# Global queries of two batches instead of one at the end, value copies on the chip for eight pairs, and a new order

## The chip, the cores and the metric

The kernel runs on one core of a Trainium2 chip. The metric is the device time of one execution in microseconds (us). In the profile the engines are PE (TensorE, matrix products), DVE (VectorE), ACT (ScalarE), POOL (GpSimd) and SP (SyncE, which here does nothing but issue DMA transfers).

## The reference

Two layers in float32. The first is attention over 8 batches and 8 heads of width 64, with 32 global and 512 local tokens per head: a global query sees everything, a local query sees the 32 global keys and the local keys at most 32 positions away. The second layer multiplies two projections of the result and sends the product through two more weights.

```python
s_g   = scale * q_g @ concat(k_g, k_l).T          # 32 x 544 a head
out_g = softmax(s_g) @ concat(v_g, v_l)
s_ll  = where(|i - j| <= 32, scale * q_l @ k_l.T, -1e9)
out_l = softmax(concat(scale * q_l @ k_g.T, s_ll)) @ concat(v_g, v_l)
x     = concat(out_g, out_l) as (8 * 544 tokens, 512)
out   = (((x @ w1) * (x @ w2)) @ w3) @ w_out      # w1, w2 512x1024, w3 1024x1024, w_out 1024x512
```

## The kernel before, in words

**Weights.** `w3 @ w_out` is folded into one 1024x512 matrix on the chip: `fold` (L690 to L693), 64 steps of two matmuls each, into 8 tiles that are then split in a high and a low float32r part (`w34h`, `w34l`, L695). The weights come packed (`fetch`, 512 KB a tile for w3 and wo); each tile is unpacked (`unit`) by a shift on DVE (L603), an activation on ACT (L605) and a shift-and-or on DVE (L607), where w1 and w2 are split as well (by further `unit` steps).

**Pairs.** A pair m is two heads of one batch (m = 0 to 31, batch m // 4). For each pair SP loads q, k and v. `kc` (L320 to L324) spreads K into shifted windows in two copies; `vc` (L309 to L314) spreads the global V in two copies. The values also need V shifted by 32 rows either way: for pairs below `VC` this is made on the chip by four copies `vs` (L297 to L304, two large ones of 32x1536 and two small ones of 32x384 elements), for the others by four more DMA transfers (L292 to L295). `s` is the scores (L348, 64 short matmuls), `mm` and `ex` the minimum on DVE and the exponential on ACT, eight of each. For pairs below `TP` the weights are turned by PE (`tp`) and copied out (`pt`); for the others by DVE and a round trip through DRAM (`tn`, `po`, `pi`). `v` is the values (L400, 64 short matmuls), `nm` the division; for pairs below `XT` `xt` turns the result on PE (four transposes), for the others DVE and DRAM do (`vn`, `vw`, `vi`). `xh` and `xl` split it in two float32r parts, the input of the second layer.

**Global queries.** They are worked two pairs at a time (u = m // 2): `sg` scores (L471, 48 matmuls), `gq`, `gr`, `ge` minimum and exponential, `gt`, `go`, `gi` the turn through DRAM (`gi` is the read-back, L381), `vg` values (L500 and L505), `gn`, `gd` division and write-out. They need K and V of their pairs on the chip. They run for m from `LATE` to 31 together with the pairs; those of the first `LATE` pairs are done at the end of the program as m = 32 and up, for which K and V are loaded and spread again (`keys`). When all are written, `gin` reads the global tokens back, and `gxh` and `gxl` split them.

**Second layer.** 17 blocks k of at most 256 tokens, 4 groups each. `first` (L546 to L548) is a step of 12 gate matmuls, in which w1 and w2 meet x; `ga`, `gb_`, `gh`, `gl` copy one half, multiply and split (ACT and DVE); `second` (L576 to L578) sends the product through the folded matrix; `out` and `store` write it out. Block 15 is the global tokens, block 16 the last local ones.

**What sets the order.** Nothing is scheduled at run time. `ORDER_OF` gives each step of each kind a position in one common order of the program, 0 to 2516; a letter A, D or P before it chooses ACT, DVE or POOL. Each engine carries out its own steps in rising position and waits wherever a step's input, or the buffer that it writes to, is not ready. SP issues all transfers in this order too, so one that waits holds up those behind it. Buffers are rings of fixed length: K 2, V 3, q 2, raw weights 3. `warm` is 20 matmul records on a cleared tile (`clear`, L250) that have no use in the result. The lines that set how much runs where:

```python
LAG, TP, XT, LATE, VC = 1, 4, 4, 4, 4                      # L27
        nc.sync.dma_start(V[32:64], src)                   # L289
        if m < VC:
            return
        nc.sync.dma_start(V[0:32, 1:4], src[:, 0:3])       # L292, and three more
        for part in range(4 * (m < VC)):                   # L745
            add(("vs", m, part), "POOL ACT DVE", [("load", "v", m)], shift_v, m, part)
    for m in range(NM + LATE):                             # L972, NM = 32 pairs
        if m < NM:
            pair(m)
        if m >= LATE:
            global_pair(m)
```

## Time and profile before

| | |
|---|---|
| median of 3 runs | 761.49 us (755.45 to 762.23) |
| the profiled execution | 756.57 us, of which its span is 754.8 us |
| PE busy | 736.7 us (98% of the span) |
| weight loads of PE (overlapping) | 644.5 us (85%) |
| DVE busy | 424.5 us (56%) |
| ACT busy | 272.9 us (36%) |
| POOL busy | 116.8 us (15%) |
| moved by DMA | 133.95 MB, 177 GB/s on the mean |
| instructions | 24101 |

The span runs from the first to the last instruction that the profile shows; the execution's own time is 1.8 us longer. A share of busy time is a mean over stages with different limits, so it says which engine to look at and not where the time goes. A busy PE is one that has matmuls in its pipe; since their ends are modelled, it may still run below its peak. A line of a group such as "x40 | 16.0, 404 | 1.1 <-DVE mn L355 1.0" reads: 40 instructions, 16.0 us busy, 404 ns each on the mean, 1.1 us of idle time of the engine ahead of them, 1.0 of which ended when DVE wrote `mn` on L355.

### The profile page before, as it was taken

The page shows a single profiled execution, that of the slowest core. Times are in us where ns is not written, and L with a number is a line of the kernel's source. Part 1 is how long each engine was busy: PE and PEld are TensorE (multiplying, and loading weights), DVE is VectorE, ACT ScalarE, POOL GpSimd, SP SyncE. Part 2 cuts the span into 40 slices and gives each one's busy share as a digit, 9 for nine tenths or more (in the row PEclk, how much of TensorE's full clock was granted, in tenths as well). Part 3 has the DMA queues.
Part 4 walks back from the last instruction along what each step waited for, and adds up shares of the span by engine and source line. Part 5 has one row for each costly group of instructions (what it writes and reads, how often), then busy time and mean ns, then how long its engine had stood idle before and what let it go on. Part 6 is the DMA issues. An engine that isn't in the chain of part 4 may idle for free.

```text
span 754.8 us, 24101 instructions
## 1 busy us (share of the span) xinstructions
PE 736.7 (98%) x10036; PEld 644.5 (85%) x10036; DVE 424.5 (56%) x1264; ACT 272.9 (36%) x839; POOL 116.8 (15%) x174
## 2 busy tenths in 40 slices
PE   4989999999999999999999999999999999999998
PEld 3345598999998998989989999999988999999997
DVE  4787887756555457555675645656554455424232
ACT  4677876533244232213334333442323321210000
POOL 2034533110102110200201120102100111110000
PEclk9999999999999999999999999999999999999999
DMA  8997787786678483957575677667593848210000
GB/s 282 303 291 273 179 244 218 213 245 198 173 198 238 127 219 93 256 144 193 144 218 171 169 209 229 198 182 196 144 244 104 242 138 218 76 45 29 1 29 29
DMA packets 98037, 133.95 MB, mean 177 GB/s; under 512 B 15848, under 2 KB 58472, under 8 KB 97928
## 3 DMA queue, kind: packets, MB, share of 16 engines
q1 hardware_dynamic: 97928, 132.41, 61.6%
q8 instruction: 79, 1.29, 0.8%
q14 instruction: 30, 0.25, 0.1%
HBM read 94.62 MB, written 37.75 MB: 175 GB/s over the span
## 4 chain that ended last, share of the span: by engine, by line
PE 94%; DMA 3%; DVE 1%; issue 1%; ACT 0%; SPq 0%; DVEq 0%; ACTq 0%
PE bp L546 9%; PE ap L546 9%; PE acc L576 9%; PE bp L547 8%; PE acc L578 8%; PE bp L548 8%; PE acc L577 8%; PE ap L548 8%; PE ap L547 8%; PE w L693 5%; PE s L348 4%; PE v L400 4%; PE sg L471 2%; DMA raw_wo<-in_wo_t_dram 2%; PE gx L500 2%; DMA raw_w<-in_w_t_dram 2%
## 5 line engine op out<-in xcount | busy, mean ns | idle before, releaser
L546 PE MATMUL bp<-x,w12h 128*128 128x256 f32 x512 | 144.5, 282 | 0.0
L546 PE MATMUL ap<-x,w12h 128*128 128x256 f32 x512 | 144.3, 282 | 0.0
L547 PE MATMUL bp<-x,w12h 128*128 128x256 f32 x512 | 142.4, 278 | 0.2 <-issue 0.2
L548 PE MATMUL bp<-x,w12l 128*128 128x256 f32 x512 | 142.2, 278 | 0.0
L547 PE MATMUL ap<-x,w12h 128*128 128x256 f32 x512 | 142.2, 278 | 0.0
L548 PE MATMUL ap<-x,w12l 128*128 128x256 f32 x512 | 142.1, 277 | 0.0
L360 ACT ACTIVATE P<-P,mn 128x128 f32<-128x128 f32 x256 | 100.7, 396 | 44.4 <-issue 24.3
L546 PEld LDWEIGHTS bp<-x,w12h 128*128 128x128 f32 x512 | 96.2, 188 | 4.7 <-issue 2.4
L546 PEld LDWEIGHTS ap<-x,w12h 128*128 128x128 f32 x512 | 96.1, 188 | 4.1 <-issue 1.6
L547 PEld LDWEIGHTS bp<-x,w12h 128*128 128x128 f32 x512 | 96.3, 188 | 2.0 <-issue 0.4
L547 PEld LDWEIGHTS ap<-x,w12h 128*128 128x128 f32 x512 | 96.2, 188 | 1.6
L548 PEld LDWEIGHTS ap<-x,w12l 128*128 128x128 f32 x512 | 96.5, 189 | 0.0
L548 PEld LDWEIGHTS bp<-x,w12l 128*128 128x128 f32 x512 | 96.5, 189 | 0.0
L355 DVE CUSTOM_DVE_ANT_0 P<-s,cs 128x128 f32<-128x128 f32 x256 | 62.7, 281 | 35.1 <-PE s L348 34.5
L693 PE MATMUL w<-wo,w3f 128*128 128x512 f32 x128 | 59.5, 603 | 5.3 <-issue 3.0
L314 POOL COPY V<-vg 32x1024 f32<-32x1024 f32 x35 | 37.0, 1065 | 135.4 <-PE gx L500 68.3
L693 PEld LDWEIGHTS w<-wo,w3f 128*128 128x128 f32 x128 | 22.7, 190 | 32.3 <-issue 24.5
L360 ACT ACTIVATION_READ_ACCUMULATOR P<-P,mn 128x1 f32 x256 | 48.9, 191 | 0.0
L348 PE MATMUL s<-K,q 64*32 64x128 f32 x2048 | 37.8, 278 | 8.9 <-DVE w3f L607 8.8
L348 PEld LDWEIGHTS s<-K,q 64*32 64x32 f32 x2048 | 29.1, 107 | 18.3 <-issue 13.6
L324 POOL COPY K<-K 128x480 f32<-128x480 f32 x26 | 16.1, 632 | 136.4 <-DMA K<-in_kp_t_dram 129.4
L416 DVE TENSOR_TENSOR vo<-v,si 128x512 f32<-128x512 f32 x32 | 22.0, 687 | 24.8 <-PE v L400 21.4
(786 smaller groups left out, 1355.7 us busy)
## 6 DMA issues: line engine op xcount, KB each, us to landing
Pd<-P SPq DMA_DIRECT2D x112, 128.0 KB, 2.6
Pt<-Pd SPq DMA_DIRECT2D x28, 512.0 KB, 4.9
raw_w<-in_w_t_dram SPq DMA_DIRECT2D x24, 512.0 KB, 5.8
V<-in_v_t_dram SPq DMA_DIRECT2D x64, 192.0 KB, 4.3
K<-in_kp_t_dram SPq DMA_DIRECT2D x36, 272.0 KB, 3.9
V<-in_v_t_dram SPq DMA_DIRECT2D x36, 256.0 KB, 4.0
out_dram<-o SPq DMA_DIRECT2D x34, 256.0 KB, 3.3
q<-in_q_t_dram SPq DMA_DIRECT2D x32, 256.0 KB, 4.3
```

Of the source, the lines that this page charges most:

```text
L314: (nc.scalar.copy if eng is nc.scalar else eng.tensor_copy)(to, src)
L348: nc.tensor.matmul(block(st[:, h], x, 128 * g), q[64 * h : 64 * h + 64, c : c + 32], window(m, h, 4 * g + x), start=True, stop=True, skip_ ...
L355: nc.vector.tensor_tensor_reduce(T["P", m][:, :, h, g], chunks(T["s", m][:, h, 128 * g : 128 * g + 128]), chunks(masks[g]), -0.125, 3.0e38 ...
L360: nc.scalar.activation(P, P, AF.Exp, bias=T["mn", m][:, g, h : h + 1], scale=-1.0, accum_out=T["sm", m][:, g, h : h + 1])
L400: nc.tensor.matmul(vt[32 * x : 32 * x + 32, g, h], t[:, x, h, g], Vs[m % NV][:, x, h, g], start=True, stop=True, skip_group_check=True)
L546: nc.tensor.matmul(d, wh[:, k, c, :], x[:, 0, 0:w], start=(k == m % 2 == 0), stop=False, skip_group_check=True)
L547: nc.tensor.matmul(d, wh[:, k, c, :], x[:, 1, 0:w], start=False, stop=False, skip_group_check=True)
L548: nc.tensor.matmul(d, wl[:, k, c, :], x[:, 0, 0:w], start=False, stop=(k == 3), skip_group_check=True)
L576: nc.tensor.matmul(a, gh[:, m % 2, sl], wh, start=(m == 0), stop=False)
L577: nc.tensor.matmul(a, gh[:, m % 2, sl], wl, start=False, stop=False)
L578: nc.tensor.matmul(a, gl[:, m % 2, sl], wh, start=False, stop=(m == 7))
L693: nc.tensor.matmul(T["w34", t], T["w3f", t, j // 4][:, j % 4], T["wo"][:, j], start=(j == 0), stop=(j == 7))
```

## The change

Two constants change, and with them how many steps of some kinds there are, so the whole of `ORDER_OF` is written anew. No function changes.

- `LATE` 4 to 8: the global queries of batches 0 and 1 (u = 16 to 19), instead of those of batch 0 alone (u = 16, 17), stand at the end. The K, V and global V of eight pairs instead of four are loaded and spread a second time, and qg of batch 1 is loaded late.
- `VC` 4 to 8: pairs 4 to 7 get their shifted V by four copies each instead of four transfers. Reloaded pairs (m of 32 and up) still take the transfers.
- The new order has 2558 steps (2517 before): SP 377 (368), POOL 174 (152), ACT 554 (550), DVE 870 (864), PE 583 (583). Engine letters move too: `vs` is now on ACT 15 times, DVE 4, POOL 13 (8, 2, 6); `kc` 24, 21, 35 (29, 17, 26); `vc` 30, 20, 30 (21, 16, 35); `xl` is 22 on DVE and 42 on POOL (37 and 27).

```diff
-LAG, TP, XT, LATE, VC = 1, 4, 4, 4, 4
+LAG, TP, XT, LATE, VC = 1, 4, 4, 8, 8
...
-    clear="13 2 44",
-    edges="20",
-    warm="22",
...
-    vs="A149 P174 P173 A140 A120 D111 A157 D131 A200 A191 P253 P236 A351 P292 P248 A288",
...
-    sg="440 628 741 885 994 1131 1266 1386 1525 1653 1788 1906 2033 2170 2245 2313",
...
-    gi="609 740 853 1021 1094 1256 1405 1542 1641 1740 1898 2021 2159 2251 2305 2359",
-    vg="659 776 886 1048 1136 1279 1449 1573 1652 1758 1917 2057 2171 2276 2316 2360",
...
-    gin="2371 2376 2401 2404",
...
+    clear="12 4 24",
+    edges="27",
+    warm="18",
...
+    vs="A136 D145 A61 P213 A105 P221 D124 D87 P260 A208 A258 P198 A327 P372 P344 D362 P474 A504 P416 A396 P493 A489  "
+    "P423 P532 P664 A540 A639 A546 A691 A628 A680 P602",
...
+    v="217 265 335 392 514 594 685 741 800 866 905 973 1071 1096 1164 1242 1312 1387 1459 1500 1580 1670 1704 1774  "
...
+    sg="743 870 1009 1125 1238 1395 1517 1638 1787 1897 2025 2153 2218 2279 2331 2385",
...
+    gi="825 966 1122 1227 1357 1491 1659 1721 1903 2021 2125 2234 2290 2337 2376 2411",
+    vg="865 983 1126 1240 1389 1501 1663 1770 1942 2050 2152 2242 2297 2339 2393 2424",
...
+    gin="2439 2445 2452 2459",
```

The new lists of `vs` stand pair after pair, four to a pair, so those of pair 4 are P474, A504, P416 and A396, and its values stand at 514. Four stretches of the orders, position and step (a step is named by its kind, then pair or tile, then part):

```
SP before   0 w3.0.0  1 k.0  4 vg.0  5 w3.3.0  6 constants  7 q.0  8 k.1  9 w3.1.0  10 wo.0  18 w3.2.0  29 wo.4  30 wo.1
SP after    0 w3.0.0  2 wo.0  3 vg.0  6 k.0  7 k.1  13 constants  16 q.0  17 w3.3.0  20 w3.1.0  23 w3.2.0  26 wo.1  28 wo.2
PE before   19 s.0  22 warm  48 fold.3.0  49 fold.0.0  57 fold.1.0  ...  185 s.2  192 v.0  ...  440 sg.2  442 first.0.0.0
PE after    18 warm  31 fold.0.0  32 s.0  54 fold.1.0  56 fold.1.1  ...  200 s.2  209 fold.4.1  217 v.0  ...  454 first.0.0.0
ACT after   473 ga.0  477 kc.7.0  482 unit.w12s.4.2.4  484 ex  485 ex  489 vs.5.1  490 ex  502 unit.w12s.5.0.2  504 vs.4.1
PE end, before   2313 sg.17  2316 vg.16  ...  2360 vg.17  ...  2461 first.16.0.0
PE end, after    2385 sg.19  2393 vg.18  ...  2424 vg.19  ...  2465 first.15.0.0
```

Between sg.19 and vg.19 PE has seven steps of `first`, four of `second` and vg.18; between sg.17 and vg.17 before it had seven and five, and vg.16. The sizes of the transfers at the start: a w3 or wo tile 512 KB, k 272, q 256, constants 112, vg 64.

## Rows read from the trace of the kernel before

**Rows 1.** Busy time by stretch (start:end, length; PE, weight loads, DVE, ACT, POOL; clock, DMA, GB/s)
```profile
20.00:40.00 20.00, 18.82 (x104) 8.07 (x103) 14.41 (x41) 13.72 (x34) 1.79 (x2) 1.00 0.98 311
40.00:60.00 20.00, 16.83 (x237) 9.30 (x237) 15.33 (x44) 15.43 (x36) 8.34 (x11) 1.00 0.95 285
60.00:80.00 20.00, 20.00 (x243) 10.70 (x242) 16.94 (x51) 14.56 (x41) 8.00 (x8) 1.00 0.65 229
...
140.00:700.00 560.00, 559.76 (x8086) 512.82 (x8075) 304.70 (x914) 173.54 (x580) 70.20 (x100) 1.00 0.63 173
...
740.00:754.80 14.80, 11.19 (x73) 9.84 (x71) 3.99 (x6) 1.17 (x2) 0.00 (x0) 1.00 0.10 37
sum 754.80, PE 736.68 PEld 644.45 DVE 424.48 ACT 272.86 POOL 116.81; mean PE 61.39 PEld 53.70 DVE 35.37 ACT 22.74 POOL 9.73
...
0.00:94.00 94.00, 79.73 (x884) 42.58 (x884) 67.49 (x206) 64.42 (x155) 30.80 (x52) 1.00 0.85 266
```

**Rows 2.** PE in order of time, 0 to 60 us (start, length, step [idle before <-releaser])
```profile
8.85 1.96 PE L348 MATMUL s<-K,q 64*32 64x128 f32 x64 [8.85 <-DVE w3f L607]
10.74 4.21 PE L861 MATMUL warm<-og 128*128 128x128 f32 x20
...
48.80 1.10 PE L400 MATMUL v<-V,Pt 128*32 128x64 f32 x64
53.48 2.41 PE L693 MATMUL w<-wo,w3f 128*128 128x512 f32 x5 [2.96 <-issue]
```

**Rows 3.** Groups of instructions by line, PE, from the start to 46.7 us
```profile
L693 PE MATMUL w<-wo,w3f 128*128 128x512 f32 x60 | 27.6, 604 | 2.4 <-DVE wo L607 2.0 <-DVE w3f L607 0.4
```

**Rows 4.** PE in order of time, around the first gate matmul
```profile
93.25 0.94 PE L471 MATMUL sg<-K,qg 64*32 64x128 f32 x48
94.12 0.39 PE L546 MATMUL ap<-x,w12h 128*128 128x256 f32 x1
...
95.60 0.28 PE L546 MATMUL ap<-x,w12h 128*128 128x256 f32 x1
```

**Rows 5.** POOL and DVE in order of time, at the start
```profile
7.27 0.21 POOL L250 MEMSET og<- 128x128 f32 x1
8.15 0.69 DVE L607 SCALAR_TENSOR_TENSOR w3f<-raw_w 128x512 int32<-128x512 int32 x1 [0.38 <-ACT raw_w L605]
14.44 0.43 DVE L603 TENSOR_SCALAR raw_wo<-raw_wo 128x512 int32<-128x512 int32 x1 [0.38 <-DMA raw_wo<-in_wo_t_dram]
```

**Rows 6.** The chain that ended last: a run of folds (start, length, what)
```profile
59.15 9.64 PE w L693 x22
```

**Rows 7.** Groups of instructions by form, ACT, from the start to 94.1 us
```profile
L360 ACT ACTIVATE P<-P,mn 128x128 f32<-128x128 f32 x40 | 16.0, 404 | 1.1 <-DVE mn L355 1.0
L304 ACT COPY V<-V 32x1536 f32<-32x1536 f32 x5 | 7.4, 1473 | 0.1
L324 ACT COPY K<-K 128x480 f32<-128x480 f32 x6 | 3.4, 585 | 3.7 <-DMA K<-in_kp_t_dram 3.7
L314 ACT COPY V<-vg 32x1024 f32<-32x1024 f32 x3 | 3.1, 1042 | 0.1
```

**Rows 8.** K and V copies on DVE and POOL (ns least/median/most; then in time)
```profile
L324 DVE COPY K<-K x17: 361/426/1682, 5.8 to 617.7; 128x480 f32<-128x480 f32 x17
41.14 1.68 DVE L324 COPY K<-K 128x480 f32<-128x480 f32 x1
40.08 2.47 POOL L304 COPY V<-V 32x384 f32<-32x384 f32 x2
```

**Rows 9.** The last global pair, in time, and its read-backs (KB each, us to landing)
```profile
633.69 0.94 PE L471 MATMUL sg<-K,qg 64*32 64x128 f32 x48
646.49 0.34 SPq L381 DMA_DIRECT2D Gt<-Gd  x1
652.43 0.88 PE L500 MATMUL gx<-V,Gt 128*32 128x64 f32 x48
Gt<-Gd SPq DMA_DIRECT2D x16, 384.0 KB, 4.2
```

More of the change, by code (lines that the diff above doesn't have):

```diff
@@ L171 @@
-    "2500 2507",
-    second="505 531 559 582 624 626 678 689 728 729 756 774 783 789 823 827 867 868 888 897 913 914 953 968 1001 1006  "
[6 rows of a table removed]
-    out="A695 A727 A829 A849 A977 D997 A1130 D1140 D1230 A1234 A1371 A1381 D1492 A1500 D1626 A1630 A1752 A1759 A1907  "
-    "A1921 A2058 A2066 A2158 A2167 A2267 A2287 A2365 A2367 A2425 D2429 A2476 D2480 D2510 A2515",
-    store="797 834 851 1022 1053 1000 1200 1154 1369 1404 1374 1454 1514 1660 1738 1781 1845 2044 2027 2074 2132 2131  "
-    "2227 2178 2321 2422 2421 2370 2449 2488 2511 2496 2514 2516",
+    load="13 16 6 42 3 41 7 66 161 115 157 211 156 290 301 210 338 273 330 288 405 389 371 427 428 426 570 586 501  "
[5 rows of a table added]
@@ new lines @@
+    clear="12 4 24",
+    edges="27",
+    warm="18",
+    fetch="0 2 20 23 17 26 28 48 55 51 65 70 102 119 89 127 132 144 151 140 160 175 207 216 176 226 281 289 320 357  "
+    "331 394 224 272 283 407 483 494 500 498 521 547 558 544 587 607 634 603",
+    unit="15 1 19 8 9 14 30 21 34 44 39 46 29 22 33 38 37 43 53 40 68 82 62 83 92 88 96 75 73 81 91 85 98 97 101 108  "
[7 rows of a table added]
+    fold="31 63 100 106 120 147 154 158 54 56 93 121 137 178 179 197 57 94 95 107 125 164 165 167 104 112 122 126 138  "
+    "139 148 153 180 209 218 225 241 245 274 282 219 246 264 266 293 294 303 307 336 376 377 391 404 409 435 448  "
@@ new lines @@
+    "1820 1896 1943 2023 2073 2169 2237 2278",
+    iv="170 232 298 360 446 545 638 694 749 814 889 956 1000 1095 1154 1189 1255 1327 1419 1479 1527 1602 1684 1729  "
+    "1786 1830 1929 1976 2056 2116 2215 2258",
+    nm="220 284 342 418 529 614 693 746 809 884 911 979 1080 1119 1176 1251 1314 1411 1462 1525 1587 1677 1712 1782  "
+    "1825 1923 1955 2029 2112 2212 2248 2287",
+    xt="250 325 351 421",
+    xh="A291 D271 A328 A329 A368 A395 A433 A466 P681 P655 A717 A702 P795 A838 P807 D848 A958 A934 P997 A982 P1016  "
@@ new lines @@
+    "1984 2069 2159 2214 2269",
+    vn="534 633 709 754 847 886 917 985 1081 1136 1206 1266 1323 1441 1469 1530 1588 1682 1741 1788 1851 1926 1977  "
+    "2030 2187 2225 2249 2311",
+    vw="548 649 729 764 873 903 972 988 1111 1156 1225 1284 1358 1454 1520 1539 1597 1706 1780 1811 1876 1944 2022  "
+    "2063 2201 2235 2252 2330",
+    vi="635 665 730 784 933 971 990 1025 1155 1179 1285 1309 1384 1467 1523 1568 1633 1727 1804 1821 1907 1957 2037  "
+    "2105 2221 2247 2304 2356",
+    sg="743 870 1009 1125 1238 1395 1517 1638 1787 1897 2025 2153 2218 2279 2331 2385",
@@ new lines @@
+    gxl="D2442 P2453 D2458 D2464",
+    first="454 468 461 467 486 511 515 517 553 575 588 595 615 660 648 668 678 679 695 697 706 713 723 724 750 756 770  "
[12 rows of a table added]
+    ga="A473 A518 A600 D669 A699 A719 D767 A793 A823 A850 A879 A913 D938 D970 A1021 A1052 A1084 D1138 D1158 A1194  "
[3 rows of a table added]
+    gb_="479 552 611 673 708 739 774 803 830 861 887 921 942 1002 1026 1060 1085 1143 1173 1207 1239 1267 1299 1335  "
+    "1355 1383 1424 1449 1477 1512 1540 1573 1631 1661 1689 1728 1763 1795 1823 1856 1902 1924 1978 2015 2039  "
@@ new lines @@
+    "2538 2547",
+    second="499 522 581 598 629 630 688 690 718 725 757 762 802 805 827 831 859 863 876 888 909 916 940 941 996 1003  "
[6 rows of a table added]
+    out="D692 D701 A834 A844 A944 A960 A1103 A1108 A1258 A1269 D1354 D1371 A1492 A1493 D1647 A1652 A1769 A1771 A1913  "
+    "D1917 A2049 D2055 A2170 A2173 A2291 D2293 A2408 A2410 A2463 A2466 A2511 A2513 D2552 A2555",
+    store="753 936 893 892 1053 989 1121 1322 1321 1306 1367 1532 1634 1542 1758 1888 1873 1939 2046 2068 2086 2088  "
+    "2224 2396 2342 2416 2414 2456 2512 2545 2553 2554 2556 2557",
```

104 lines of the change are left out of this document (39 added, 65 removed), and 127 rows, old and new, of tables (ex, first, ga, gh).

## The prediction, made before the change was run

> **What bounds the kernel now.** I read the page first: its busy table puts TensorE (PE) far ahead of the other engines, 736.68 us of matmuls in 754.8 [rows 1]. A busy share alone does not say that an engine is the limit, so the next view is the busy time by stretch [rows 1]. The reader is to see three parts in it. Up to 60 us PE has gaps (18.82 of 20, 16.83 of 20) while the DMA engines stand at 0.98 and 0.95: weights are being fetched. From 60 us on PE has none worth the name (559.76 of 560 between 140 and 700). At the end 3.6 us are left for the last output. The granted clock is 1.00 in every stretch, the upper of the two levels, so no part of the forecast is about the clock.
>
> The time order of PE's start [rows 2] shows the gaps themselves: nothing before 8.85 us, and 2.96 us ahead of 53.48 whose releaser is "issue", that is, nothing the profile shows. The first gate matmul comes at 94.12 us [rows 4], and from there on PE is never without work. So time can be won only before 94.12 us; it can be lost anywhere.
>
> **What the change does to PE's work: nothing.** Both orders hold the same PE steps (32 scores, 32 values, 64 folds of two matmuls, 272 gate groups, 16 global scores and values). The rest is moved or added on other engines, so the sum consists of waits. I follow the new order through its critical places.
>
> **Start, up to 46.5 us.** PE now begins with the warm-up, behind POOL's clearing of its operand (7.27 + 0.21 = 7.5 us [rows 5]) instead of behind the first scores (8.85): 1.4 us earlier. It runs 4.21 us [rows 2]; one fold and the scores of pair 0 bring it to about 13.7 us. The next fold needs the first w3 tile of row 1 (fetch w3.1.0). In the new SyncE (SP) order 3,024 KB are issued up to it; in the old order just as many stand up to the first wo tile (512+272+64+512+112+256+272+512+512), and VectorE (DVE) could start on that at 14.44 us [rows 5]. Two unpackings follow on ScalarE (ACT) and two on DVE, about 0.69 us each [rows 5], so the fold starts near 17.2 us: PE waits 3.5 us, and the earlier start is spent. I went on like this by hand (512 KB in 1.7 us at the 311 GB/s of [rows 1], unpackings in DVE's queue order): the weight tiles that end the waits are unpacked at 26.5, 29.6, 31.7, 34.3, 37.0 and 38.4 us, and at 46.5 us 31 folds are done. Before, by 46.76 us, it was 30 folds (60 matmuls [rows 3]) and eight transposes, which is the same work. Gain: 0.3 us. Bounds: the 1.4 us won or lost.
>
> **From there to the first gate matmul.** Before: 94.12 - 46.76 = 47.4 us, of which 0.94 us is a global step of the second batch [rows 4], now moved to the end (not saved), and 2.96 us the unexplained gap. The other 43.5 us are dense work (folds at 2 x 0.438 us, from 9.64 us for 22 matmuls [rows 6], scores, values, transposes); the new order has one fold less and eight transposes more, so 43.5 us again: 46.5 + 43.5 = 90.0 us if the gap does not come back. It came right behind scores 2 and values 0, 64 short matmuls each, 1.10 us a step [rows 2]. In the new order the same two stand in the same place (33 folds ahead of scores 2, not 31), with one fold of 0.86 us between. I let the gap come back less that fold: 2.1 us; bounds 0 and 2.96. The comparison is then 92.1 against 94.12 - 0.94 = 93.2 us. Gain of both parts together: 1.1 us, bounds 0.2 and 3.2, and 1.4 us more either way from the first.
>
> The Trainium skill, "Runtime: NRT & Kernel Launch" (Instruction fetch mechanics), says that instructions come in 16 KiB blocks of 256 and that crossing into the next block is mostly hidden. No row names that gap as a fetch. By that page alone no gap would be expected and the sum would be 2.1 us lower; by the row it is.
>
> What covers this part is ACT and DVE. ACT is busy 64.42 us of the first 94 [rows 1]. Ahead of the first gate matmul it gets one K spread (0.59), four spreads of global V (1.04 each), two copies of transposes (about the same 0.59) and three exponentials (0.40) more, one large V copy (1.47) and one cast (0.59) fewer [rows 7]: +5.1 us, 69.5 of 92 us, 76%. Its densest stretch shown is 15.43 of 20, 77% [rows 1]. So the cover holds, barely; I price it at nothing here and come back to it.
>
> **The first block.** The 16 shifted V transfers of pairs 4 to 7 leave SP; PE waited for none of them. In their place 16 copies come: eight large (1.47 us on ACT [rows 7]) and eight small (a large and a small one together 2.47 us on POOL [rows 8]). PE works strictly in order, so values 4 to 7 now wait for a copy's queue, not for a landing. Counting from the first gate matmul, the gate of group 0 starts on ACT at 5.6 us (four gate groups, each 12 matmuls in some 1.4 us [rows 4]); behind it ACT has a K spread, a cast, three exponentials, one large copy, one unpacking and then the copy for values 4, which ends near 11.8 us. PE gets there at 11.3 us: 0.5 us of waiting. The first output matmuls stand only two PE steps (2.5 us) behind their last gate matmul, while gate copy, product and two splits take four times some 0.69 us (the size of the unpacking in [rows 5]) plus, an estimate, 0.3 us of hand-over: another 0.5 us. Values 5 to 7 have 30 positions and more behind their copies, save a few small ones. Sum: 1.0 us; bounds 0 and the second rival below.
>
> **The middle** I cost at nothing: its cover is PE's own 559.76 of 560 us [rows 1]; two global groups leave DVE and ACT near 100 us.
>
> **The end.** Four pairs more are reloaded (K 272 KB, V in five transfers, 4 MB in all); the DMA engines stand at 0.63 on the mean of 140 to 700 us [rows 1]. The eight K and eight V spreads are some 13 us over three engines that have room. The chain of a global pair is what can stop PE. Before, the last one went from its scores at 633.69 to the read-back issued at 646.49, plus 0.34 and 4.2 us of landing: 17.3 us; its values ran only at 652.43 [rows 9]. The new order leaves PE work of 17.2 us between the last global scores and their values (seven gate groups and four output groups of about 1.4, the scores 0.94, one values step 0.88): 0.1 us short. Behind the values some 19 us of PE work stand ahead of the global block, for a write-out, four read-backs (two of them behind the first two tiles' splits) and the splits; I take 0.2 us for that. Sum 0.3 us, bounds 0 and 3.
>
> **Sum.** -1.1 + 1.0 + 0.3 = +0.2 us. Against the profiled execution (756.57 us: its span 754.8 and 1.8 around it) that is 756.8. This execution lies 4.9 us below the median of the runs shown (761.49; 755.45 to 762.23); nothing tells which level the median of the changed kernel falls on, so I add half the distance, 2.4 us: 759.
>
> **Rivals.** *A real gain* (chance 0.17). The gap does not return (2.1), values 4 and the first outputs find their data ready (1.0), and the early start counts (1.4): 756.8 - 4.5 = 752.3, with the half distance 754.7. For it: PE stands empty for 3.2 us between 40 and 60 us alone [rows 1]. Against it: weights arrive at the DMA engines' pace, which the order does not raise.
>
> *Slower: the V copies hold up PE in the first block* (0.12). If ACT needs more than the 77% it has shown, each of values 4 to 7 waits for one large copy and one spread, 1.47 + 1.04 = 2.5 us; four times that is 10 us: 766.8, with the half distance 769. It decides from the point where the copy for values 4 starts on ACT later than about 10 us after the first gate matmul. Against it: in that block ACT loses three global exponentials and some spreads, and its sum is about unchanged.
>
> *Slower: POOL and DVE get into each other's way* (0.04). DVE's K copy takes 0.43 us in the middle case and 1.68 at most, and the long one ran beside two V copies on POOL [rows 8]. Seven more V copies on POOL at 1.25 us each are 8.8 us of DVE time: 765.6 if all of it were on the path, but DVE had 3 of 20 us free even between 60 and 80 us [rows 1]. The Trainium skill's "SBUF — State Buffer" (Who interferes with whom) has the rule: a DVE copy in a two-port mode and a POOL instruction exclude each other for the whole instruction. The row of the K copy agrees.
>
> *Slower: the end* (0.05). Each of four global chains is 1.5 us late because V and K of the next pair share the SP queue with its read-back: +6, 762.8. *As forecast*: 0.62.
>
> **How the numbers follow.** Runs of this kernel tell about 1% from no change: below 753.9 and above 769.1 against the median. Half of the gain case and a part of the forecast (a low level with a small gain) lie below: 0.17. Two thirds of the slow first block, part of the other two and a tail of the forecast lie above: 0.13. Within: 0.70. The range, 751 to 769, goes from the gain case at a low level to the slow block and leaves out about 2 in 10.
>
> **What would show it.** Right: warm-up near 7.5 us and a wait of about 3 us before the second fold; the first gate matmul near 92 us; an "issue" gap near 50 us; PE at 20 of 20 in every stretch from 60 to 740. Wrong: a first gate matmul before 90 or after 95; values matmuls waiting for ACT or POOL copies of V between 92 and 140 us; PE waiting in the last 120 us for a read-back.

## The result and the profile after

The changed kernel takes 764.98 us (median of 17 runs, 760.32 to 767.14) against 758.21 us (17 runs, 755.45 to 762.88) of the kernel before: a ratio of 1.0083, 95% interval 1.0066 to 1.0101. So it is slower, by 6.8 us in the medians and by 0.8% in the ratio. One run of h_best, below, took 1390.99 us at a mean granted clock of 0.875 and is left out of that kernel's figures. The profiled executions lie 9.9 us apart (766.43 against 756.57), because the one of before is 1.6 us faster than its median and the one of after 1.5 us slower. The account below is of the 9.9.

Busy time by stretch of the changed kernel (start:end, length; PE, weight loads, DVE, ACT, POOL; clock, DMA share, GB/s):

```profile
20.00:40.00 20.00, 18.07 (x98) 7.87 (x99) 13.74 (x50) 16.20 (x34) 0.00 (x0) 0.85 0.95 280
40.00:60.00 20.00, 20.00 (x181) 10.11 (x180) 17.67 (x42) 15.67 (x40) 5.80 (x7) 1.00 0.89 296
60.00:80.00 20.00, 18.63 (x305) 10.52 (x304) 17.23 (x61) 15.94 (x49) 10.59 (x10) 1.00 0.88 264
...
100.00:120.00 20.00, 19.32 (x307) 17.48 (x306) 15.70 (x58) 16.39 (x40) 11.18 (x16) 1.00 0.73 220
120.00:140.00 20.00, 17.09 (x235) 15.23 (x233) 16.04 (x48) 13.78 (x44) 8.57 (x13) 1.00 0.85 230
```

The last two stretches of the kernel before:

```profile
100.00:120.00 20.00, 20.00 (x311) 17.86 (x310) 16.93 (x57) 14.47 (x40) 7.61 (x12) 1.00 0.85 264
120.00:140.00 20.00, 20.00 (x371) 18.05 (x373) 15.03 (x54) 12.80 (x44) 5.87 (x7) 1.00 0.75 216
```

Beside these and [rows 1], three things differ. The clock column has a 0.85 where before had 1.00 throughout. The stretch 40 to 60, which had the hole before, is full (20.00 against 16.83). And PE has holes at 60 to 80 (18.63) and in the first block of the second layer, up to 140 (19.32 and 17.09), where it had none; the DMA share at 60 to 80 is 0.88 where it was 0.65.

What PE waited for in the changed kernel (engine, line, releaser: us in total, times, longest; its lines are 4 higher than those of before):

```profile
PE warm L865 <- POOL og L254: 7.9, 1, 7.9
PE w L697 <- DVE w3f L611: 4.4, 2, 3.8
PE v L404 <- DMA Pt<-Pd: 2.9, 2, 2.2
PE w L697 <- DVE wo L611: 2.0, 1, 2.0
PE s L352 <- DMA q<-in_q_t_dram: 1.0, 1, 1.0
PE ap L550 <- ACT w12h L444: 0.8, 1, 0.8
PE ap L550 <- ACT as__1163 L444: 0.7, 1, 0.7
PE acc L580 <- DVE gh__10163 L444: 0.6, 1, 0.6
```

These are many small waits, and a wait does not show what a slower matmul costs. So I also took the time from the start of each PE step to the start of the next, less the usual time of a step of that kind (its median: a gate group 1.386 us, an output group 1.375, scores 1.086, values 1.031, a fold 0.859, global scores 0.868). What is left is lost time, and the two kernels have the same PE steps. Us lost, worked out from the traces:

| | 0–40 | 40–60 | 60–100 | 100–140 | 140–720 | 720–end | sum |
|---|---|---|---|---|---|---|---|
| before | 13.6 | 3.7 | 0.8 | 1.2 | 8.1 | -1.6 | 25.8 |
| after | 17.7 | 0.9 | 2.5 | 5.5 | 11.5 | -2.3 | 35.7 |

Lost time is more than idle time: a step whose matmuls run slower or are issued late counts too, so before has some as well, and the start counts whole. The differences are +4.1, -2.9, +1.7, +4.3, +3.4 and -0.7, in sum 9.9 us (before rounding). No single wait carries the loss.

A profile is one execution. Worked out in the same way, the first five columns are 17.6, 0.6, 2.8, 6.7 and 10.9 in a second execution of the changed kernel (a_again, below) and 14.6, 1.4, 1.2, 1.6 and 10.3 in b_vc8, which has the PE order of before. The start and the first block stand out in both pairs. The 3.4 us between 140 and 720 are less sure: there the second pair differs by 0.6, with a hole of 1.73 us in b_vc8 on the other side.

### The profile page after: what moved, and what is told of

It reads as the page before. It is cut to its first block, busy times and chain, and to the rows that moved or that the text cites. A ratio compares the mean times of both kernels' runs of the same rounds, so it can differ in the third digit from the quotient of the medians.

```text
span 764.7 us, 24186 instructions
## 1 busy us (share of the span) xinstructions
PE 740.0 (97%) x10036; PEld 645.9 (84%) x10036; DVE 433.7 (57%) x1270; ACT 288.4 (38%) x843; POOL 130.7 (17%) x196
## 4 chain that ended last, share of the span: by engine, by line
PE 86%; DMA 7%; DVE 3%; ACT 1%; issue 1%; SPq 0%; POOL 0%; DVEq 0%; ACTq 0%; POOLq 0%
PE ap L550 8%; PE acc L580 8%; PE bp L550 8%; PE bp L551 8%; PE bp L552 8%; PE acc L582 8%; PE ap L552 8%; PE ap L551 8%; PE acc L581 8%; PE v L404 4%; PE s L352 4%; PE w L697 4%; PE sg L475 2%; PE gx L504 2%; DMA raw_wo<-in_wo_t_dram 1%; DMA V<-in_v_t_dram 1%
## 5 line engine op out<-in xcount | busy, mean ns | idle before, releaser
L697 PE MATMUL w<-wo,w3f 128*128 128x512 f32 x128 | 61.7, 621 | 6.4 <-DVE w3f L611 4.4
L318 POOL COPY V<-vg 32x1024 f32<-32x1024 f32 x30 | 32.0, 1070 | 123.4 <-PE gx L504 45.5
L328 POOL COPY K<-K 128x480 f32<-128x480 f32 x35 | 21.0, 608 | 148.2 <-DMA K<-in_kp_t_dram 80.2
L447 POOL TENSOR_TENSOR x<-xr,x 128x256 fp32r<-128x256 f32 x42 | 30.9, 741 | 63.1 <-DVE x L444 26.6
L404 PEld LDWEIGHTS v<-V,Pt 128*32 128x32 f32 x2048 | 30.1, 110 | 10.3 <-issue 5.2
```

Of the source, the lines that this page charges most:

```text
L318: (nc.scalar.copy if eng is nc.scalar else eng.tensor_copy)(to, src)
L404: nc.tensor.matmul(vt[32 * x : 32 * x + 32, g, h], t[:, x, h, g], Vs[m % NV][:, x, h, g], start=True, stop=True, skip_group_check=True)
L697: nc.tensor.matmul(T["w34", t], T["w3f", t, j // 4][:, j % 4], T["wo"][:, j], start=(j == 0), stop=(j == 7))
```

## The experiments

The theories were: the **start** (the granted clock falls in the new waits and the folds after them run slowly), the **gap** (the time of before's 2.96 us hole is given back later), the **copies** (sixteen V copies hold up the first block), and the **order** (the new places of transfers and steps, whatever the copies do). Each run is compared with the kernel before on the same chip; its median in those groups of runs was 755.31 to 756.22. The changed kernel itself came to 1.0083 and, run again in another group, to 1.0135, with intervals that do not overlap, so ratios of different groups are compared with care. Edits of orders are given as steps on an engine, since the lists of positions shift as a whole.

### Which half of the program is it? h_start and h_rest

```diff
 h_start:  order and constants of after up to first.0.0.0, of before from there
 h_rest:   order of before up to first.0.0.0, of after from there (LATE 8, VC 8)
```

> The changed kernel's order up to the first gate matmul, then the order and the constants of the kernel before (LATE and VC 4; four steps that cannot stand so early keep their old place). Theory 1 (the start: PE waits 3.8 us for w3.1.0 behind the warm-up, its granted clock falls to about half between 16 and 28 us, and the folds run late from there): slower than before by 3 to 6 us, the clock below 1.00 in 16 to 28 us, first gate matmul at 95 us or later although the gap of 3 us near 50 us is gone. Theory 2 (the first block and the end: values 5 waits for its turned weights, the last global pairs are late): within 1.5 us of before, and the 4 us lost ahead of 40 us come back by 94 us.

> The order of the kernel before up to the first gate matmul, then the changed kernel's order and constants (LATE and VC 8). Theory 1 (the start is most of the loss): at most 3 us slower than before, clock 1.00 throughout. Theory 2 (first block and end): 4 to 7 us slower than before, with waits of PE for a read-back between 100 and 140 us.

h_start 765.36 us, 1.0123 (1.0094 to 1.0153); h_rest 765.24, 1.0132 (1.0084 to 1.0180). Either half makes the kernel slower, and both together cost no more than either alone. In h_start the joint, the place where the two orders meet, has a price of its own: the first global scores of the old rest come too early for the new start.

```profile
PE sg L471 <- DVE mn L355: 4.8, 1, 4.8
```

That row is from the waits of PE in h_start; without it about half of h_start's 10 us is left. In h_rest the first block loses 7.0 us by the account behind the old start, so the block's loss is not only a late start handed on: its first gate matmul came at 92.43 us.

### Does the clock matter? e_fill, e_hold, and the changed kernel again

```diff
 e_fill:  PE warm, fold.0.0, s.0,
+         fill(9): nc.tensor.matmul(T["fill"][:, 0:128], og, og), 9 times
          fold.1.0,
+         fill(4)
          fold.1.1
```

> The changed kernel with 9 more unused matmuls on the cleared tile behind scores 0 and 4 behind the first fold of tile 1, that is, in the two stretches (14.4 to 18.2 and 19.4 to 21.3 us) in which PE had nothing to do. No other step moves. Theory 1 with the clock as its cause: granted clock 1.00 from the first matmul on, the six folds from 21.3 us take 2.6 us and not 5.1, and the time is 2 to 5 us below the changed kernel's (before + 2 to + 4). Rival (the weight tiles set the pace anyway): clock 1.00, but PE reaches the next weight tile earlier and waits there, and the time is within 1 us of the changed kernel's.

770.25 us, 1.0180 (1.0148 to 1.0211). The added matmuls were meant to keep PE at work in the two waits. They lengthened PE's program by 52 instructions, and something else moved with it: PE stood for 2.40 and 1.89 us with the releaser "issue" in blocks 2 and 3, behind the short matmuls of global steps. In its profile the clock stayed at 1.00 and the first gate matmul came at 91.94 us, 3.7 us earlier than in the changed kernel, but the edit had a second effect, so the run does not answer the question. The next one keeps the number of instructions:

```diff
-        for _ in range(10):      # warm
+        for _ in range(6):
+        if m == 0: hold(3)                # behind the scores of pair 0
+        if (t, j) == (1, 0): hold(1)      # behind fold.1.0
+    def hold(n):                          # n times a 128x512 product, not used
+        nc.tensor.matmul(T["hold"], T["w3f", 0, 0][:, 0], T["wo"][:, 0], ...)
```

> The changed kernel with PE kept at work in its two early waits, at the same number of PE instructions: the warm-up is 6 products instead of 10, three unused products of the size of a fold stand behind scores 0 and one behind the first fold of tile 1. No other step moves, and no later PE instruction has another number in the program. If the granted clock is the cause of a part of the loss: clock 1.00 from the first fold on in most runs, first gate matmul at 92 to 93 us instead of 95.6, and 2 to 4 us below the changed kernel in the same job. Rival (the weights set the pace of the start, or the first block gives the gain back): clock 1.00, within 1 us of the changed kernel in the same job.

> The changed kernel again, beside e_hold on the same chip. 1.007 to 1.010 of the kernel before, as its first runs had it; its mean granted clock between 0.992 and 0.999, and the slower the run the lower the clock.

e_hold 764.23 us, 1.0101 (1.0074 to 1.0127); the changed kernel itself beside it 766.04, 1.0135 (1.0110 to 1.0161). Busy time by stretches of 4 us, the changed kernel first and e_hold second:

```profile
16.00:20.00 4.00, 1.21 (x2) 0.30 (x2) 1.69 (x5) 1.31 (x4) 0.00 (x0) 0.88 0.94 260
20.00:24.00 4.00, 2.67 (x3) 1.12 (x4) 3.65 (x20) 3.16 (x8) 0.00 (x0) 0.50 1.04 244
24.00:28.00 4.00, 4.00 (x70) 1.90 (x69) 1.08 (x6) 2.97 (x6) 0.00 (x0) 0.77 1.06 326
```

```profile
16.00:20.00 4.00, 2.90 (x7) 0.79 (x5) 2.23 (x6) 1.44 (x3) 0.00 (x0) 1.00 1.00 287
20.00:24.00 4.00, 3.77 (x59) 1.71 (x65) 3.50 (x19) 2.09 (x7) 0.00 (x0) 1.00 1.02 287
```

The clock column goes to 0.50, the lower level of 1.2 GHz, in the changed kernel, and stays at 1.00 in e_hold. The time order of PE shows what that did to the folds, first in the changed kernel and then in e_hold (start, length, step, idle before it):

```profile
18.17 1.21 PE L697 MATMUL w<-wo,w3f 128*128 128x512 f32 x2 [3.81 <-DVE w3f L611]
21.34 5.07 PE L697 MATMUL w<-wo,w3f 128*128 128x512 f32 x6 [1.96 <-DVE wo L611]
```

```profile
20.20 3.13 PE L699 MATMUL w<-wo,w3f 128*128 128x512 f32 x6 [1.05 <-DVE wo L613]
29.60 2.84 PE L699 MATMUL w<-wo,w3f 128*128 128x512 f32 x6 [0.68 <-DVE wo L613]
33.77 6.70 PE L699 MATMUL w<-wo,w3f 128*128 128x512 f32 x15 [1.33 <-DVE w3f L613]
```

Six fold matmuls take 5.07 us, most of it at the lower level, and 3.13 at the upper. But e_hold then waits 0.68 and 1.33 us for the next weight tiles, and its first gate matmul comes at 94.12 us, against 95.60 in the changed kernel and 94.89 when that was run again. Of the 1.9 us saved on the six folds 1.5 or 0.8 are left there, by these single executions; the rest goes to the new waits. In the medians the held clock is worth 1.8 us, with intervals that overlap. Over the 17 runs of the changed kernel the time falls as the mean granted clock rises (a line through them ends at 760.3 us at 1.0), but e_hold ran at a mean clock of 0.998 to 1.000 and still took 764.23. The reading that fits both is that early weights give a high clock and a short time together, and that most of the slope is not the clock's doing; when the weights arrive cannot be set, so this is not shown directly.

### Is it the long wait for the second fold? e_fold

```diff
-PE  warm, fold.0.0, s.0, fold.1.0, fold.1.1, ... (fold.3.0 at 104)
+PE  warm, fold.0.0, s.0, fold.3.0, fold.1.0, fold.1.1, ...
```

> The changed kernel with one step moved: the first fold of tile 3, whose weights are on the chip early, stands right behind scores 0 instead of 70 positions later, in the wait of 3.8 us. Theory 1: the wait shrinks by 0.9 us in two pieces, the clock falls later or less, 1 to 4 us below the changed kernel. Rival (pace of the weights): at most 0.9 us below it, with the same clock.

762.65 us, 1.0094 (1.0060 to 1.0128). In the profiled execution the second fold waited 1.62 us, the clock held, 13.7 us are lost up to 40 us, as in before, and the first gate matmul comes at 90.28 us, 5.3 us earlier than in the changed kernel. That the moved fold did this is not shown. f_v5, below, has the same order as e_fold up to that matmul, step for step on every engine, and h_block nearly so; there the same fold waited 3.08 and 2.62 us, the clock fell, and the first gate matmul came at 94.91 and 92.92 us. The stretch 20 to 24 us in e_fold, f_v5 and h_block:

```profile
20.00:24.00 4.00, 4.00 (x71) 2.04 (x71) 2.25 (x14) 2.71 (x10) 0.00 (x0) 1.00 1.02 359
20.00:24.00 4.00, 2.37 (x3) 1.13 (x4) 3.55 (x16) 3.18 (x8) 0.00 (x0) 0.50 1.04 233
20.00:24.00 4.00, 3.91 (x5) 1.80 (x6) 3.38 (x19) 2.47 (x8) 0.00 (x0) 0.50 1.03 316
```

So one order of the start differs by 4.6 us between two executions (on two chips), more than the 4.1 us that the account puts on the start, and the median of e_fold lies within the interval of the changed kernel's first runs.

In e_fold the block then takes longer: from the first gate matmul to first.1.0.0, the first step of the next block, 43.2 us instead of 41.7 (before 36.5). Of 5.3 us won ahead, the profiled execution of e_fold is only 3.8 us faster than that of the changed kernel.

### Is it the copies? f_vc4 and b_vc8

```diff
 f_vc4:  e_fold with
-LAG, TP, XT, LATE, VC = 1, 4, 4, 8, 8
+LAG, TP, XT, LATE, VC = 1, 4, 4, 8, 4      # the transfers again for pairs 4 to 7
 b_vc8:  the kernel before with
-LAG, TP, XT, LATE, VC = 1, 4, 4, 4, 4
+LAG, TP, XT, LATE, VC = 1, 4, 4, 4, 8      # 16 copies, 4 to 64 positions ahead of v.4 to v.7
```

> The kernel of e_fold (the changed kernel with the first fold of tile 3 brought forward, whose clock holds) with VC back at 4: pairs 4 to 7 take their shifted V by four transfers again, all other steps in their order. Theory A (the V copies make ACT, DVE and POOL late in the first block, which lost 6.0 us of PE time between 100 and 140 us there and 1.2 in before): the block loses 3 us or less, the time is 2 to 4 us below e_fold. Theory B (the new order places the steps of PE too close to their inputs): within 1.5 us of e_fold, the same waits in the same places.

> The kernel before with VC 8 alone: the 16 shifted-V transfers of pairs 4 to 7 become copies on the engines that the changed kernel gives them, put into the old order 40 to 60 positions ahead of the values that need them; every other step stands where it stood. Theory A (the copies hold up the first block): 2 us or more slower than before, with waits of PE for copies or casts between 100 and 145 us. Theory B (the new order of the other steps does): within 1 us of before, the block loses 2 us or less.

f_vc4 766.77 us, 1.0139 (1.0112 to 1.0166): without the copies the block's loss stays (5.3 us), but values 5 now waits 2.18 us for a transfer of V, so this run alone would not clear the copies. b_vc8 756.26, 1.0009 (0.9988 to 1.0031): with the copies, on the engines that the change gives them, the old order loses nothing. Its first block by stretch, the kernel of the copies alone:

```profile
100.00:120.00 20.00, 19.89 (x310) 17.65 (x309) 17.75 (x58) 18.07 (x44) 10.05 (x16) 1.00 0.79 239
120.00:140.00 20.00, 20.00 (x405) 17.98 (x404) 16.93 (x52) 14.60 (x46) 5.77 (x7) 1.00 0.78 215
```

ACT is busy 18.07 of 20 us, 90%, and PE still runs 19.89 and 20.00. So the copies by themselves are not the cause, and 77% was no limit of ACT's.

### Is it the gap? b_gap and b_gap3

```diff
 b_gap:   before with
-PE  s.2, v.0, ..., fold.1.7
+PE  s.2, fold.1.7, v.0, ...          (b_gap3: three folds, v.0 behind fold.4.1)
```

> The kernel before with values 0 moved one fold later, so that scores 2 and values 0 do not stand next to each other. If the gap of 2.96 us near 50 us comes from two steps of 64 short matmuls in a row (theory): the gap is gone or below 1 us, 2 to 3 us faster than before. If it belongs to the place in the program or to the DMA traffic there: the gap stays, same time within 0.7 us.

> The kernel before with values 0 three folds later than scores 2 and two steps of folds further than in b_gap, in search of a version that beats both. If the gap near 50 us is PE waiting for its own instructions behind two steps of 64 short matmuls, spreading them over 2.6 us of folds leaves a gap of 0.5 us or less there: 1 to 3 us faster than before. Rival: in the mean over the executions the gap is small or is made up for by the weights, and the time is that of before within 0.7 us, as in b_gap.

b_gap 756.58 us, 1.0008 (0.9986 to 1.0030); b_gap3 756.85, 1.0017 (1.0002 to 1.0033). In b_gap the hole moved into values 0 and shrank:

```profile
54.38 0.24 PE L400 MATMUL v<-V,Pt 128*32 128x64 f32 x1 [1.24 <-issue]
```

Moving the hole of the profiled execution is worth nothing in the medians. b_vc8 has the same PE program as before up to there and no hole at 50 us: it does not come in every execution, so it could not be a gain to count on.

### Where in the rest? h_mid, h_block, h_late

```diff
 h_mid:    order of b_vc8 up to first.2.0.0, then of after (LATE 8, VC 8)
 h_block:  start of e_fold, blocks 0 and 1 of b_vc8, then after
 h_late:   order of before up to first.10.0.0, then of after (LATE 8, VC 4)
```

> The order of b_vc8 (the old one with the copies) up to the first gate step of block 2, near 172 us, then the changed kernel's order, with LATE and VC 8. It holds the old start and the old first block. If the rest of the new order costs what the profile of the changed kernel shows behind 140 us (3.4 us more than before, 1.2 of it in block 14): 2 to 4 us slower than before. Rival (the new order costs only in its first 140 us): within 1 us of before.

> The start of e_fold up to the first gate matmul, the order of b_vc8 for blocks 0 and 1, then the changed kernel's order, LATE and VC 8. Against e_fold only the order inside the first two blocks differs. Theory B (the order of the block): block 2 starts 2 to 4 us earlier than in e_fold (173.5 us), and the time is 2 to 4 us below e_fold's ratio of 1.009. Rival (the weights of w1 and w2 arrive when they arrive): block 2 starts within 1 us of e_fold's.

> The kernel before up to the first gate step of block 10 (near 490 us), then the changed kernel's order, with LATE 8 and VC 4: four more pairs are loaded and spread again and two more global pairs stand at the end. It shows what the late part costs by itself. Profile of the changed kernel: 0.9 us at values 29, 1.2 us at the output groups of block 14, so 1 to 2.5 us slower than before. Rival (nothing, the engines have room): within 0.7 us, less the two global steps of the first 490 us that are then done later.

h_mid 765.24 us, 1.0099 (1.0064 to 1.0134); h_block 766.24, 1.0131 (1.0104 to 1.0158); h_late 768.52, 1.0158 (1.0131 to 1.0184). From the first gate matmul to the next block the old order needs 36.8 us with the copies in b_vc8, 37.8 in h_mid and 39.0 in h_block; the new one 40.7 to 44.6 in all the kernels that have it. The stretches do not hold quite the same steps: h_mid and h_block lack a global step of 0.87 us. Net of the usual time of their steps b_vc8 loses 1.3 us there, h_mid 3.2 and h_block 4.4, and with the old order behind the new start h_start 2.5 and h_best, below, 4.6; the new order loses 5.0 to 8.8. So most of the block's loss goes with its order, and a part of it with what stands ahead. But giving the block its old order back did not make the kernel as fast as before. h_mid and h_block have a wait of their own at the second joint (values 8; 4.2 us lost there and in the step behind it), and h_mid's profiled execution, 759.56 us, is the fastest of its six, with a first gate matmul at 87.68: its account alone would have misled me. h_late loses 25.1 us between 140 and 720 us where before loses 8.1, and most of that is a thing that I had not looked for (its PE waits):

```profile
PE gx L507 <- issue: 1.9, 1, 1.9
PE v L402 <- issue: 1.5, 1, 1.5
PE ap L548 <- issue: 1.4, 1, 1.4
PE acc L578 <- issue: 1.2, 1, 1.2
PE sg L473 <- issue: 0.9, 1, 0.9
PE bp L550 <- issue: 0.9, 1, 0.9
```

Six holes, some 8 us. More on them in the last section. They make the sum over h_late no measure of the last blocks' order. LATE 8 by itself in the old order was not run, so what the four more pairs at the end cost alone is not shown.

### The block's own wait, and a mixture: f_v5 and h_best

```diff
 f_v5:    e_fold with
-PE  ..., first.0.4.1, v.5, ..., second.0.4, ...
+PE  ..., first.0.4.1, ..., second.0.4, v.5, ...
 h_best:  start of e_fold, then the rest of before (LATE 4, VC 4), sg.2 behind first.0.1.1
```

> The kernel of e_fold with one step moved: values 5, which waited 2.1 us for the read-back of its turned weights, stands behind the output group second.0.4 as it nearly does in the kernel before (three PE steps, some 4.2 us, later); its division follows it. Theory B: the wait of 2.1 us and part of those right behind it (0.6 and 1.0) go, 1.5 to 3.5 us below e_fold. Theory A: another wait takes its place, within 1 us of e_fold.

> The start of e_fold up to the first gate matmul, then the order and the constants of the kernel before (LATE and VC 4), with the global scores of pair 4 and 5 four gate groups later than in h_start, where they waited 4.8 us. If the new start is the better one once its clock holds, and the loss lies behind the first gate matmul: first gate matmul near 90 us, first block as in before (2 us lost or less), 1 to 4 us faster than before. Rival (an earlier start is given back in the first block, whose weights arrive when they arrive): same as before within 1 us, with 4 us or more lost between 100 and 140 us.

f_v5 768.12 us, 1.0151 (1.0121 to 1.0181): the wait of values 5 is gone, and the account shows 2.2 us lost at second.0.4 and 2.05 at first.0.7.0 in its place (less than 0.4 and 1.0 there in the changed kernel). h_best 761.24, 1.0065 (1.0042 to 1.0088): the early start with the old rest comes to the first gate matmul at 91.14 us, 2.1 us ahead of before net of its global step, and is slower than before all the same; it loses 2.2 us at scores 6, and 41.0 us up to the next block. An early start is no gain if what follows is not ready for it.

### A transfer in the wrong place: e_hold_pi

```diff
 e_hold_pi:  e_hold with
-SP  ..., load v, load k.32, pi.29, ...
+SP  ..., load v, pi.29, load k.32, ...
```

> The kernel of e_hold with one transfer moved: the load of K for the first pair that is loaded a second time (k.32) stands behind the read-back of pair 29 (pi.29) instead of three transfers ahead of it. In the changed kernel that load waits for a K buffer until the global scores of pairs 30 and 31, and the read-back waits behind it on SP's queue. If this is the cause of the wait of values 29 (0.7 to 1.8 us in all kernels with the new end): the wait is gone, the read-back is issued 10 us earlier, and the time is 0.5 to 1.5 us below e_hold's ratio of 1.010. Rival (the read-back is late for another reason, or the load of K is then late for the global pair): the wait stays, or one of the same size comes up within the next 60 us.

760.73 us, 1.0079 (1.0064 to 1.0094), where e_hold had 764.23, 1.0101 (1.0074 to 1.0127). SP's own order around this place, the changed kernel first and e_hold_pi second (start, length until issued):

```profile
571.64 1.25 SPq L299 DMA_DIRECT2D V<-in_v_t_dram  x1
583.61 0.35 SPq L285 DMA_DIRECT2D K<-in_kp_t_dram  x1
584.00 0.43 SPq L385 DMA_DIRECT2D Pt<-Pd  x1
```

```profile
565.70 1.11 SPq L298 DMA_DIRECT2D V<-in_v_t_dram  x1
566.85 0.58 SPq L386 DMA_DIRECT2D Pt<-Pd  x1
577.96 0.83 SPq L284 DMA_DIRECT2D K<-in_kp_t_dram  x2
```

The waits of SP in the changed kernel, 565 to 590 us, name what the load of K on L285 waited for:

```profile
SPq L285 <- PE sg L475: 10.8, 1, 10.8
```

k.32 is the second load of K of pair 0. It needs a K buffer that the global scores of the last pairs still use, and pi.29, the read-back for values 29, stands behind it though it needs no such buffer. In the changed kernel it goes out at 584.00 and values 29 loses 0.9 us (1.8 in e_hold, 2.2 to 2.6 in h_rest and h_late); in e_hold_pi it goes out at 566.85 and less than 0.4 is lost there. The waits of PE for read-backs, e_hold first and e_hold_pi second:

```profile
PE v L406 <- DMA Pt<-Pd: 3.3, 2, 1.7
```

```profile
PE v L405 <- DMA Pt<-Pd: 0.5, 1, 0.5
```

Only one of e_hold's two waits in that row is that of values 29; the other, about as long, is that of values 5, far ahead of the edit. By the account e_hold_pi loses 1.6 us less between 140 and 720 us, and the ratios differ by about as much (0.22%). They come from different groups of runs and their intervals overlap, so the gain in time is not shown by itself: the profiled execution of e_hold_pi is 4.5 us faster, but 2.0 of these it had at the first gate matmul (92.09 against 94.12 us), before anything differs. This is the one edit that takes away a wait and brings up no other. No version was faster than the kernel before.

## Why the prediction was wrong

The time, 764.98 us, lies in the range (751 to 769) but outside the likeliest case, and slower is certain. By the account of the profiled executions the sum was not +0.2 but +9.9 us, and nearly every term was too small. Common to most of them is one step: the waits of the new order were priced with the cover that the old order gave, and where the old order had no wait the new one was put at nothing. The 2.4 us added for the level of the median are not the failure: the median of before came to 758.21 us, so the sum of +0.2 would have been 758.4.

**Start: the step "31 folds at 46.5 us" failed.** The warm-up came at 7.86 us (predicted 7.5) and the second fold waited 3.81 us (predicted 3.5), so the two ends of that step were right. The 31st fold ended at 50.9 us. The sentence that failed is "no part of the forecast is about the clock": it was read from a kernel whose folds follow straight behind the 4.21 us of warm-up [rows 2], while the changed one has one fold and the scores between and then stands idle for 3.8 and 2.0 us. (The old start is not safe from this either: in h_rest the clock fell to 0.50 behind a wait of 2.66 us.) The hand count also priced every fold at the upper level. Part of the loss is the weights' pace, which differs between executions: the first gate matmul came at 95.60 and 94.89 us in two executions of the changed kernel, and it is 94.12 in before and 93.15 in b_vc8, which have the same start. Predicted gain 0.3, measured loss 4.1; the bound of 1.4 was too narrow, narrower than what one order of the start varies by (4.6 us in e_fold and f_v5). How much of the 4.1 belongs to the order, to the clock and to the execution stays open; in the medians the held clock was worth 1.8 us.

**Gap: +2.1 us predicted to return, 0 returned.** In its place the changed kernel has dense work, in time order on PE:

```profile
55.53 1.10 PE L404 MATMUL v<-V,Pt 128*32 128x64 f32 x64
56.56 1.98 PE L697 MATMUL w<-wo,w3f 128*128 128x512 f32 x4
```

This gives 2.9 us back, within the bound of 2.96, and in the gain rival's favour. The first gate matmul is at 95.60 instead of 92.1 us, 2.4 us behind the 93.2 that before has net of its global step; what the gap gave, the start and the next stretch took. The 2.96 us were also read from one execution: by b_vc8 and b_gap there was little of them to win in the medians.

**From the gap to the gate: the step "the cover holds" failed, on an engine I did not check.** I counted ACT and DVE. Scores 4 waited 1.0 us, by the profile for a transfer (its q). The DMA share there is 0.88 and was 0.65 [rows 1]; between 58 and 80 us SP issues 5.4 MB of loads instead of 5.0. I had not followed the transfers past the first weights.

**First block: 1.0 us predicted, 4.3 measured.** Neither of the two waits that were priced came: the first output matmul (105.19 us) and values 4 (108.15) start without an idle time before them. Other waits came, and none for a V copy; the first below is gate group 2's for the copy `as` on ACT. The changed kernel's PE in time order:

```profile
102.49 0.38 PE L550 MATMUL ap<-x,w12h 128*128 128x256 f32 x1 [0.68 <-ACT as__1163 L444]
122.66 1.10 PE L404 MATMUL v<-V,Pt 128*32 128x64 f32 x64 [2.15 <-DMA Pt<-Pd]
134.25 0.39 PE L550 MATMUL ap<-x,w12h 128*128 128x256 f32 x1 [0.75 <-ACT w12h L444]
```

The 2.15 us are for a read-back of pair 5, which SP issues behind other transfers and which lands late:

```profile
112.75 1.84 SPq L437 DMA_DIRECT2D vd<-vo  x4
115.15 0.43 SPq L385 DMA_DIRECT2D Pt<-Pd  x1
```

It took 7.5 us to land; the median of such read-backs is 4.3. The 0.75 us are for the last unpacked tile of w1 and w2, whose high part ACT has ready at 134.2 us and DVE its low part at 134.7 (126.9 in before). I had said of pairs 4 to 7 that only their V had moved. Their read-backs and the last weight tiles had moved as well, and I followed the copies alone. The rival "the V copies hold up PE" named the right place and the wrong cause; b_vc8 and f_vc4 together clear the copies. How the remaining loss of the block divides among its late chains is open: f_v5 showed that moving one wait brings up the next.

**Rival of POOL and DVE: there, and seen once ahead of a wait of PE.** DVE and POOL in time order, in the changed kernel:

```profile
131.30 2.44 DVE L611 SCALAR_TENSOR_TENSOR raw_w12s<-raw_w12s 128x256 int32<-128x256 int32 x2
131.91 1.54 POOL L308 COPY V<-V 32x1536 f32<-32x1536 f32 x1
```

Two unpackings that usually take 0.43 us each take 2.44 us together, and the 0.75 us wait for an unpacked tile follows. The second alone starts at 132.1 us, inside the V copy on POOL, takes 1.68 us and ends 0.3 us behind the copy. The Trainium skill, "SBUF — State Buffer" (Who interferes with whom), calls the ports that the two engines share an exclusive lock; the trace agrees, since that instruction does not end before the copy has. Over the whole execution 22 instructions of DVE take over 0.25 us more than the median of their form, 12.4 us in sum, and each of them overlaps an instruction of POOL (17 and 9.1 us in before). On the path of PE the row above is worth less than a microsecond; what the others cost is not shown.

**Middle: the step "I cost at nothing" failed.** PE's 559.76 of 560 us in before is the cover of before's order; I took it for that of the new one. Lost: 3.4 us more than before. Values 29 is 0.9 of it, by the mechanism of the last rival (a K load and a read-back on one queue), but it struck a local pair's read-back, where I had put it on the global pairs'. Scores 16 is 0.6, and 1.16 is at the last output groups of block 14 (about 690 us):

```profile
691.12 0.50 PE L580 MATMUL acc<-w34h,gh__10163 128*128 128x512 f32 x1 [0.55 <-DVE gh__10163 L444]
```

Before, gate groups of the global block stood ahead of these; now the last of the global tokens are read back only from 689.66 us on, too late for that, and the order gives PE nothing else there. The rest, about 1 us, is spread over many steps and stays open. The 3.4 us are of one pair of executions; the waits named are in the second execution of the changed kernel too (0.7 at values 29, 0.7 in block 14).

**End: 0.3 predicted as PE's wait for the last read-backs, none seen.** The cost of a later end came ahead of it, in the 1.16 us just named.

**The chances.** "Within 1%" had 0.70 and came true by its number, not by its mechanism: that is luck. "Above 769.1" had 0.13, and the three slower rivals together 0.21. Five parts were priced, each with the cover that the old order gave it. A new order of 2558 steps against one in which PE stood still for 0.24 of 560 us had little to win there and much to lose; a part of the forecast's 0.62 belonged to "several small waits, 5 to 10 us", which was no rival of mine.

## What to carry to other kernels

Where a tuned order keeps the limiting engine at 99.9%, a change that rewrites the order must be priced wait by wait in the new order, and "nothing" is the best case there, not the middle one. Look on the queue that issues transfers for one that must wait for a buffer and stands ahead of one that need not; one pair of steps exchanged was the only edit here that removed a wait without bringing up another. A first profile of an edited start says little: look at a second execution of the same order before a wait there is put down to the edit. Time won ahead of a stage whose inputs are late on their own is given back in that stage, so measure a start by the end of the program and not by the first matmul of the next stage.

## What the hardware showed that was not expected

**Holes in PE behind short matmuls.** The holes with the releaser "issue" are read here as PE waiting for its own instructions. In h_late the six lie behind the 4761st, 7051st, 8323rd, 11123rd, 11885th and 12903rd matmul or weight load of PE; the distances are 9, 5, 11, 3 and 4 times 254.0 to 254.5. In before and in b_gap, where another step stands in the place, the hole is behind the 695th in both. In e_fill, whose 52 more instructions move every step, the two are behind the 4763rd and 5781st, within 2 of the same grid (two holes of 0.7 us in b_gap3 lie off it). The profile's table of DMA queues shows the transfers that go with it (packets, MB, share):

```profile
q8 instruction: 79, 1.29, 0.7%
```

That is 16 KB each, and in h_late one starts 0.6 to 1.6 us ahead of each hole. Four of the six lie in or right behind scores or values steps, own or global, of 48 to 64 short matmuls, two within gate groups; that of before lies behind values 0. They took 0.9 to 3.0 us, and the same place has a hole in one execution and none in another (before and b_vc8 at 50 us). The Trainium skill, "Runtime: NRT & Kernel Launch" (Instruction fetch mechanics), has instructions come in blocks of 256, which agrees with the distances, and crossing a block mostly hidden, which these holes limit: of 79 such transfers a few were not hidden here. An edit that adds a few instructions ahead moves every later crossing, as e_fill showed, and can cost more than what it tests.

**The clock at the start.** Idle times of 3.81 and 1.96 us on PE, with short work between, went with a granted clock of 0.50 and folds at 0.85 us a matmul instead of 0.52 (5.07 and 3.13 us for six). It cost less than that ratio suggests, 1.8 us in the medians with intervals that overlap; that the weights which come next set the pace is the likely reason, not a shown one.

**DVE instructions beside POOL.** Instructions of DVE that took 0.25 us or more above the median of their form, 22 in the changed kernel and 17 in before, all overlapped one of POOL, though POOL is busy for only 15 to 17% of the span.
